# A planned conformer kernel on one core: own ends for the last two chunks, VectorE's score tiles by one PSUM bank at a time, and background before products

## The chip, the cores and the metric

The kernel runs on one core of a Trainium2 chip. The metric is the device time of one execution in microseconds (us). Each kernel was executed several times; all runs quoted here (none was over 1.5% above the fastest of its kernel) can be compared with each other. The span of a profile is a little shorter than the device time of the same run (1026.3 against 1028.1 us for the kernel before).

Engines are named as the profile names them: PE (matmuls), PEld (PE's weight loads), DVE (VectorE), ACT (ScalarE), POOL (GpSimd), SP (its queue issues the stores).

## The reference

One conformer block on two sequences of 4000 tokens of width 144, four heads of 36, all in bf16:

```python
h = silu(layernorm(x) @ w_ff1a) @ w_ff1b;      x = x + 0.5 * h
q, k, v = split(layernorm(x) @ w_qkv)                       # 4 heads of 36
p = softmax(einsum('bhqd,bhkd->bhqk', q, k) * 36 ** -0.5)   # 4000 x 4000 per head
x = x + einsum('bhqk,bhkd->bhqd', p, v) @ w_o
a, b = split(layernorm(x) @ w_pw1);            h = a * sigmoid(b)
c = depthwise_conv_of_5_taps(h, dw);           x = x + silu(c) @ w_pw2
h = silu(layernorm(x) @ w_ff2a) @ w_ff2b;      x = x + 0.5 * h
return layernorm(x)
```

## The kernel before

The tokens are cut into 16 chunks of 500 (eight per sequence). The attention of a chunk walks over 63 key tiles of 64 rows, so there are 1008 score tiles. One score tile has four heads times 64 keys times 500 queries; it fills two PSUM banks (128 x 1000 numbers), and its exponential is the main work of the kernel. Everything else is called background here: the first half of a chunk (`pre`: feed-forward 1, q, k, v), and the second half (`post1`: output projection and gate; `post2`: convolution, feed-forward 2, last LayerNorm, store).

The important fact about this program is that its order is decided when it is built. A small list scheduler in Python keeps a clock for each engine, with an estimated cost for each instruction. It picks the next step, emits it, and in the end writes one fixed instruction stream per engine, with semaphores. I call that the plan. A step that the plan puts at a wrong moment stays there: the engine waits in its queue.

Six PSUM banks serve scores and background; two hold the attention's accumulators. `KEEP = 2` keeps two pairs of banks for ScalarE's score tiles. The parts that the change and the argument touch, with cuts marked:

```python
    NXN, NXT, NTH, NHT, NSW = 5, 5, 4, 3, 2      # NSW: buffers of the convolution's result
    KEEP = 2; DSLACK = 0.6; BMIN = 1.5; DRAIN = 0.6; DGAP = 5.0

    def post2(c):                                  # the second half's end, one generator per chunk
        last = c % CPB == CPB - 1
        z = yield need("pe", swp, cond=lambda: c in glu_done and (last or c + 1 in glu_done))
        ...                                        # convolution, pw2, LayerNorm, feed-forward 2, store

    def emit_S(n):                                 # one score tile: four 64x64 quadrants, two banks
        lo, hi = banks.take_pair()
        for p in range(2):
            for hh in range(2):
                op("pe", "matmul", PSV[64 * p:64 * p + 64, hi if hh else lo, 0:CH], ...)
        return lo, hi

    def dve_tile(n, lo, hi):                       # exp on VectorE, by integer operations
        z = yield need("dve", dzp, hold=True)
        for hh, bk in ((0, lo), (1, hi)):
            op("dve", "tensor_scalar", ZB[:, z, hh, :], PSV[:, bk, 0:CH], ...)
            banks.give(bk)
        ...                                        # six more steps over 128 x 1000, the last writes PT

    # pick(): which step PE gets next; o = products with V, s = scores, ok = background that fits
        if R.kind == "q" and o and (not s or ts + 0.3 < deadline):
            return o[0]
        if ok:
            return min(ok, key=lambda q: not q[2].req.hold)
        ...

    def lag():                                     # background is behind: then no VectorE tile
        ...
        back = n // NT - 0.5 * (len(glu_done) + len(post_done))
        return back > BMIN + DRAIN * (NIT - n) / NT

    def reserve():                                 # while a VectorE tile is due, a third pair is kept
        ...
        return KEEP + 1 if due else KEEP

    # when the first sequence's keys are there:
            for par in range(2):
                S.add(series(post2(c) for c in range(par, NCH, 2)), R.last, rank=2)
```

So a VectorE tile needed a whole pair beside ScalarE's two, and the second halves ran in two series: chunks 0, 2, ..., 14 and chunks 1, 3, ..., 15.

The softmax here doesn't subtract the row's maximum and nothing guards it: scores larger than these inputs give would overflow.

Of the kernel before, what the change touches and what calls it, by code (L numbers as in the profile page):

```python
# [23 lines left out]
CH = 500  # L24
KT_ROWS = 64
# [211 lines left out]
need = Req  # L237
# [71 lines left out]
def bass_standalone__conformer_family_zipformer__speech_kernel(  # L309
# [16 lines left out]
    NCH = N // CH  # L326
    CPB = T // CH
# [4 lines left out]
    R = Rec(nc)  # L332
# [3 lines left out]
    def sb(name, shape, dt=BF16):  # L336
        return nc.alloc_sbuf_tensor(name, [128] + list(shape), dt)

    NXN, NXT, NTH, NHT, NSW = 5, 5, 4, 3, 2
    NPT = 7  # L340
    NU = 5
    NAN = 5
# [3 lines left out]
    NPRE = 2  # L346
    KEEP = 2
    DSLACK = 0.6
    PRELAG = 0.5
    BMIN = 1.5  # L350
    DRAIN = 0.6
    LATE = 0.3
    DGAP = 5.0
    MAXQ = 3
    DVE_EXP = True
    VG = 7
# [564 lines left out]
    def series(gens):  # L921
        for g in gens:
            yield from g
# [26 lines left out]
    group_left = {c: NT for c in range(NCH)}  # L950
    o_count = {c: 0 for c in range(NCH)}

    def emit_S(n):
        c, t = its[n]
        b = c // CPB
        k0, q0 = t * KT_ROWS, c * CH
        lo, hi = banks.take_pair()
        kcs = {min(k0 // CH, CPB - 1), min((k0 + KT_ROWS - 1) // CH, CPB - 1)}
        for p in range(2):
            for hh in range(2):  # L960
                bk = hi if hh else lo
                op("pe", "matmul", PSV[64 * p:64 * p + 64, bk, 0:CH],
                   lhsT=KT[64 * hh:64 * hh + 64, p, b, k0:k0 + KT_ROWS], rhs=QT[64 * hh:64 * hh + 64, p, q0:q0 + CH],
                   start=True, stop=True, skip_group_check=True,
                   r=[("WKT", b * CPB + kc) for kc in kcs] + [("WQT", c), "KTZ"], w=[("ps", bk)], cost=0.0525,
                   kind="q", lat=0.2)
        return lo, hi

    def emit_exp(n, lo, hi):
# [4 lines left out]
        banks.give(hi)  # L974
        pend.append((n, pt))

    def dve_tile(n, lo, hi):
        z = yield need("dve", dzp, hold=True)
        for hh, bk in ((0, lo), (1, hi)):
            op("dve", "tensor_scalar", ZB[:, z, hh, :], PSV[:, bk, 0:CH], ATT_SCALE * LOG2E * 256.0, 127.5 * 256.0,  # L980
               op0=ALU.mult, op1=ALU.add, r=[("ps", bk), ("ZF", z)], w=[("ZB", z)], cost=c_dve(CH))
            banks.give(bk)
        zz = ZB[:, z, :, :].rearrange("p b n -> p (b n)")
        mm = MB[:, z, :, :].rearrange("p b n -> p (b n)")
        yield need("dve")
        op("dve", "tensor_scalar", mm, zz, 0xFF, 0x6400, op0=ALU.bitwise_and, op1=ALU.bitwise_or, r=[("ZB", z)],
           w=[("MB", z, 0)], cost=c_dve(2 * CH, 4))
        op("dve", "tensor_scalar", zz, zz, 1, 0x7F80, op0=ALU.logical_shift_right, op1=ALU.bitwise_and,
           r=[("ZB", z), ("MB", z, 0)], w=[("EB", z)], cost=c_dve(2 * CH, 4))
        yield need("dve")  # L990
        v = E2A / (2 * E2B)
        op("dve", "tensor_scalar", MBH[:, z, :], MBH[:, z, :], 1.0 / 256, v - 4.5, op0=ALU.mult, op1=ALU.add,
           r=[("MB", z, 0)], w=[("MB", z, 1)], cost=c_dve(2 * CH, 4))
        yield need("dve")
        op("dve", "tensor_tensor", MBH[:, z, :], MBH[:, z, :], MBH[:, z, :], op=ALU.mult, r=[("MB", z, 1)],
           w=[("MB", z, 2)], cost=c_dve(2 * CH, 2))
        yield need("dve")
        op("dve", "tensor_scalar", MBH[:, z, :], MBH[:, z, :], E2B, 1.0 - E2B * v * v, op0=ALU.mult, op1=ALU.add,
           r=[("MB", z, 2)], w=[("MB", z, 3)], cost=c_dve(2 * CH, 4))
        pt = yield need("dve", ptp)  # L1000
        op("dve", "tensor_tensor", PT[:, pt, :, :].rearrange("p b n -> p (b n)"), ZBF[:, z, :], MBH[:, z, :],
           op=ALU.mult, r=[("MB", z, 3), ("EB", z)], w=[("PT", pt), ("MB", z, 0), ("EB", z), ("ZF", z)], cost=c_dve(2 * CH, 2))
        dzp.give(z)
        pend.append((n, pt))
        live_dve[0] -= 1
# [55 lines left out]
    def pick():  # L1061
        cands = []
        ts = s_start()
        if ts is not None:
            cands.append((ts, "S", None))
        if eq and ptp.free and (len(silu_done) >= NSILU or NSILU == 0):
            n, lo, hi = eq[0]
            te = max(R.free["act"], R.ready(("ps", lo), "act"), R.ready(("ps", hi), "act"), ptp.best() + 0.045)
            cands.append((te, "E", None))
        os = [(o_start(m), m) for m in pend]  # L1070
        os = [(t, m) for t, m in os if t is not None]
        if os:
            t, m = min(os, key=lambda q: (q[0], q[1]))
            cands.append((t, "O", m))
        for th in S.threads:
            t = S.start_of(th)
            if t is not None:
                cands.append((t, "T", th))
        if not cands:
            assert banks.keep > 0, "nothing can go on"  # L1080
            banks.keep -= 1
            return pick()
        tmin = min(q[0] for q in cands)
        soon = [q for q in cands if q[0] <= tmin + 0.1]
        other = [q for q in soon if not (q[1] in "SO" or (q[1] == "T" and q[2].req.eng == "pe"))]
        pe = [q for q in cands if (q[1] in "SO" or (q[1] == "T" and q[2].req.eng == "pe"))]
        pemin = min((q[0] for q in pe), default=1e9)
        if other and (min(q[0] for q in other) <= pemin or pemin > tmin + 0.1):
            e = [q for q in other if q[1] == "E"]
            a = [q for q in other if q[1] == "T" and q[2].req.eng == "act"]  # L1090
            d = [q for q in other if q[1] == "T" and q[2].req.eng != "act"]
            if d:
                return min(d, key=lambda q: (not q[2].req.hold, q[2].rank))
            if a:
                return a[0]
            return e[0]
        near = [q for q in pe if q[0] <= pemin + PW]
        o = [q for q in near if q[1] == "O"]
        bg = [q for q in near if q[1] == "T"]
        s = [q for q in near if q[1] == "S"]  # L1100
        deadline = act_end() - 0.48
        if ts is not None:
            limit = max(deadline, ts) + (LATE if lag() else 0.0)
        else:
            limit = 1e9
        ok = [q for q in bg if max(q[0], R.free["pe"]) + q[2].req.dur + 0.095 * (R.kind != q[2].req.kind) + 0.095 <= limit]
        if R.kind == "q" and o and (not s or ts + 0.3 < deadline):
            return o[0]
        if ok:
            return min(ok, key=lambda q: not q[2].req.hold)  # L1110
        if s:
            return s[0]
        if o:
            return o[0]
        if ts is not None:
            return (ts, "S", None)
        return min(pe, key=lambda q: q[0])

    def want_dve(n):
        c, t = its[n]  # L1120
        if not DVE_EXP or live_dve[0] >= 1 or t > NT - 6 or (t < 3 and c == 0) or len(kv_done) < CPB:
            return False
        return len(eq) + banks.pairs() >= KEEP and R.free["dve"] < R.free["pe"] + DSLACK and not lag()

    last_dve = [0.0]
    front = [0.0, 0]
# [10 lines left out]
        back = n // NT - 0.5 * (len(glu_done) + len(post_done))  # L1137
        return back > BMIN + DRAIN * (NIT - n) / NT

    def reserve():  # L1140
        n = n_s[0]
        if n >= NIT or not DVE_EXP or len(kv_done) < CPB:
            return KEEP
        c, t = its[n]
        due = (live_dve[0] < 1 and t <= NT - 6 and R.free["dve"] < R.free["pe"] + DSLACK
               and R.free["pe"] > last_dve[0] + DGAP and not lag())
        return KEEP + 1 if due else KEEP

    while n_s[0] < NIT or eq or pend or live_dve[0]:
        if mode["front"] and len(kv_done) == CPB:  # L1150
            mode["front"] = False
            front[:] = [0.0, n_s[0]]
            S.add(setup_dw())
            for par in range(NPRE):
                S.add(series(pre(c, False) for c in range(CPB + par, NCH, NPRE)), R.last)
            for par in range(2):
                S.add(series(post2(c) for c in range(par, NCH, 2)), R.last, rank=2)
        banks.keep = reserve()
        t, k, v = pick()
        if k == "S":  # L1160
            n = n_s[0]
            n_s[0] += 1
            lo, hi = emit_S(n)
            if want_dve(n):
                stats["dve"] += 1
                live_dve[0] += 1
                last_dve[0] = R.free["pe"]
                S.add(dve_tile(n, lo, hi), R.last, first=True, rank=3)
            else:
                eq.append((n, lo, hi))  # L1170
        elif k == "E":
            emit_exp(*eq.pop(0))
        elif k == "O":
            pend.remove(v)
            emit_O(v)
        else:
            S.run(v)
# [43 lines left out]
```

## Time and profile before

The kernel before took 1030.56 us (median of 4 runs, 1030.09 to 1031.57). From the page of its profile: the span, busy time of each engine with its share, then groups of instructions (output from input, shapes, count; busy us and mean ns of one; idle time before them and what ended most of it), then the stores:

```profile
span 1026.3 us, 26612 instructions
...
PE 924.8 (90%) x11294; PEld 365.0 (36%) x11294; DVE 788.0 (77%) x2092; ACT 945.8 (92%) x1175; POOL 283.3 (28%) x562
...
L158 ACT ACTIVATE PT<-PS 128x1000 bf16<-128x1000 f32 x914 | 851.9, 1041 | 11.5 <-PE PS L158 9.8
L158 PE MATMUL PS<-QT,KT 64*64 64x500 bf16 x4032 | 397.4, 391 | 50.3 <-ACT PT L158 29.5
L158 DVE TENSOR_SCALAR ZB<-PS 128x500 uint16<-128x500 f32 x188 | 118.5, 672 | 33.2 <-PE PS L158 31.9
...
out_dram<-XN SPq DMA_DIRECT2D x13, 140.6 KB
out_dram<-XN SPq DMA_DIRECT2D x6, 70.3 KB
```

There are 914 exponentials on ScalarE. 852 us of busy time over 914 is 0.93 us for one in a row. VectorE read 188 half tiles out of PSUM, so it took 94 of the 1008 score tiles. Of the stores, 13 are of whole chunks and six of half chunks. The plan stores by halves only where it finishes a chunk's last feed-forward after the attention, so six halves mean that the feed-forwards of three chunks, 13, 14 and 15, ended after it.

Busy time by stretch, the second row up to the end of the last exponential and the third from there on (columns: stretch, its length, then busy us of PE, PEld, DVE, ACT and POOL with the count of instructions, PE's granted clock, share of the DMA engines, GB/s):

```profile
110.00:160.00 50.00, 44.67 (x544) 16.60 (x541) 40.76 (x115) 46.58 (x58) 15.68 (x30) 1.00 0.01 2
500.00:966.99 466.99, 428.48 (x5363) 159.43 (x5364) 366.38 (x895) 463.83 (x567) 127.04 (x251) 1.00 0.02 5
966.99:1026.32 59.33, 37.43 (x229) 23.98 (x226) 27.63 (x110) 16.59 (x31) 13.97 (x34) 0.64 0.03 8
```

Up to 966.99 us ScalarE is nearly always busy: 463.83 of 466.99 us in the long stretch. Behind that come 59.33 us in which no engine is full on average (PE is busy for 37.43 us) and PE's clock is at 0.64 on average. I call these 59.33 us the end. PE is not the limit before the end; the list of waits (total us, times, longest us) has its weight loads waiting for exponentials to free banks:

```profile
PEld PS L158 <- ACT PT L158: 268.2, 543, 1.1
```

Six lines of the timeline that show chunks in the end (start, length, instruction): the convolution (`PS<-U,DG`) of 13; the first part of 13's feed-forward (`PS<-XT,WA`); the convolution of 14; the last matmuls of 13's feed-forward (`PS<-WB,HT`); the convolution of 15 and its feed-forward, the last one:

```profile
965.63 0.77 PE L158 MATMUL PS<-U,DG 128*128 128x500 bf16 x6
...
982.53 2.70 PE L158 MATMUL PS<-XT,WA 72*128 72x500 bf16 x6
985.03 1.35 PE L158 MATMUL PS<-U,DG 128*128 128x500 bf16 x6
...
990.90 0.79 PE L158 MATMUL PS<-WB,HT 128*125 128x144 bf16 x10
...
1003.69 1.62 PE L158 MATMUL PS<-U,DG 128*128 128x500 bf16 x12
...
1012.31 3.52 PE L158 MATMUL PS<-XT,WA 72*128 72x500 bf16 x8 [0.68 <-ACT XT L158]
```

Chunk 15 convolves 18.7 us after 14, and its feed-forward at 1012.31 us has the core to itself.

| | before |
|---|---|
| device time | 1030.56 us |
| exponentials on ScalarE / score tiles on VectorE | 914 / 94 |
| end of the last exponential | 966.99 us |
| the end (from there to the end of the span) | 59.33 us |

### The profile page before, as it was taken

The page shows a single profiled execution, that of the slowest core. Times are in us where ns is not written, and L with a number is a line of the kernel's source. Part 1 is how long each engine was busy: PE and PEld are TensorE (multiplying, and loading weights), DVE is VectorE, ACT ScalarE, POOL GpSimd, SP SyncE. Part 2 cuts the span into 40 slices and gives each one's busy share as a digit, 9 for nine tenths or more (in the row PEclk, how much of TensorE's full clock was granted, in tenths as well). Part 3 has the DMA queues.
Part 4 walks back from the last instruction along what each step waited for, and adds up shares of the span by engine and source line. Part 5 has one row for each costly group of instructions (what it writes and reads, how often), then busy time and mean ns, then how long its engine had stood idle before and what let it go on. Part 6 is the DMA issues. An engine that isn't in the chain of part 4 may idle for free.

```text
span 1026.3 us, 26612 instructions
## 1 busy us (share of the span) xinstructions
PE 924.8 (90%) x11294; PEld 365.0 (36%) x11294; DVE 788.0 (77%) x2092; ACT 945.8 (92%) x1175; POOL 283.3 (28%) x562
## 2 busy tenths in 40 slices
PE   7899989998999999998999999999999988998775
PEld 4444333333334333433333332333333333343343
DVE  6976877888966987787888778968886987666843
ACT  3899999999999999999999999999999999999741
POOL 3321313114324333320422132321513212223222
PEclk9999999999999999999999999999999999999956
DMA  4000000000000000000000000000000000000000
GB/s 130 3 1 2 2 2 2 1 2 2 1 2 2 2 2 2 7 2 2 2 7 2 7 7 2 2 8 7 8 2 8 2 7 7 2 8 7 7 6 12
DMA packets 7419, 7.31 MB, mean 7 GB/s; under 512 B 2349, under 2 KB 7300, under 8 KB 7300
## 3 DMA queue, kind: packets, MB, share of 16 engines
q1 hardware_dynamic: 6144, 5.14, 1.7%
q8 instruction: 88, 1.44, 0.6%
q10 hardware_dynamic: 1156, 0.47, 0.2%
q14 instruction: 31, 0.25, 0.1%
HBM read 3.31 MB, written 2.30 MB: 5 GB/s over the span
## 4 chain that ended last, share of the span: by engine, by line
ACT 65%; PE 22%; DVE 9%; POOL 2%; issue 1%; DMA 1%; ACTq 0%; POOLq 0%; DVEq 0%
ACT PT L158 59%; PE PS L158 22%; ACT TH L158 5%; DVE ZB L158 2%; DVE ST L158 1%; DVE MB L158 1%; DVE HT L158 1%; POOL RS L158 1%; DVE X L158 1%; POOL XN L158 1%; DMA WQKV<-in_w_qkv_dram 1%; DVE XT L158 1%; DVE PT L158 0%; DVE XN L158 0%; DVE MV L158 0%
## 5 line engine op out<-in xcount | busy, mean ns | idle before, releaser
L158 ACT ACTIVATE PT<-PS 128x1000 bf16<-128x1000 f32 x914 | 851.9, 1041 | 11.5 <-PE PS L158 9.8
L158 PE MATMUL PS<-QT,KT 64*64 64x500 bf16 x4032 | 397.4, 391 | 50.3 <-ACT PT L158 29.5
L158 PE MATMUL PS<-PT,VA 64*37 64x500 bf16 x4032 | 366.1, 373 | 10.5 <-ACT PT L158 7.0
L158 POOL TENSOR_SCALAR RS<-MV 125x4 f32<-125x4 f32 (+1 forms) x160 | 46.3, 289 | 668.3 <-DVE MV L158 662.7
L158 PEld LDWEIGHTS PS<-QT,KT 64*64 64x64 bf16 x4032 | 116.8, 103 | 306.5 <-ACT PT L158 219.9
L158 DVE TENSOR_SCALAR ZB<-PS 128x500 uint16<-128x500 f32 x188 | 118.5, 672 | 33.2 <-PE PS L158 31.9
L158 PEld LDWEIGHTS PS<-PT,VA 64*37 64x37 bf16 x4032 | 105.7, 95 | 71.9 <-ACT PT L158 42.7
L158 POOL TENSOR_SCALAR XN<-X,RS 125x144 bf16<-125x144 bf16 x228 | 127.6, 572 | 5.9
L158 ACT ACTIVATE TH<-PS 128x500 bf16<-128x500 f32 (+2 forms) x195 | 103.6, 538 | 8.0 <-PE PS L158 7.7
L158 DVE SCALAR_TENSOR_TENSOR HT<-TH,PS 128x500 bf16<-128x500 bf16 (+1 forms) x135 | 82.3, 618 | 32.4 <-ACT TH L158 31.5
L158 DVE SCALAR_TENSOR_TENSOR X<-PS,X 125x288 bf16<-125x288 f32 x128 | 56.9, 452 | 58.0 <-PE PS L158 57.3
L158 POOL TENSOR_TENSOR RS<-RS,NHALF 125x4 f32<-125x4 f32 (+1 forms) x103 | 97.6, 948 | 8.6
L158 PE MATMUL PS<-XT,WA 72*128 72x500 bf16 x256 | 77.7, 402 | 5.7 <-DVE HT L158 2.3
L158 DVE TENSOR_SCALAR MB<-MB 128x1000 f16<-128x1000 f16 x188 | 78.0, 415 | 1.5
L158 DVE BATCH_NORM_STATS2 ST<-X 125x6 f32<-125x144 bf16 x320 | 75.2, 294 | 0.4
L158 DVE TENSOR_TENSOR PT<-ZB,MB 128x1000 bf16<-128x1000 bf16 x94 | 66.0, 702 | 2.2
L158 DVE TENSOR_TENSOR MB<-MB 128x1000 f16<-128x1000 f16 x94 | 63.8, 679 | 2.1
L158 PE MATMUL PS<-WB,HT 128*125 128x144 bf16 x640 | 63.1, 241 | 2.5 <-ACT HT L158 1.5
L158 PEld LDWEIGHTS PS<-WB,HT 128*125 128x125 bf16 x640 | 49.4, 143 | 37.4 <-issue 22.6
L158 PE MATMUL PS<-IDENT,XN 125*72 125x125 bf16 x512 | 44.1, 226 | 15.0 <-DVE XN L158 11.7
L158 DVE COPY XT<-PS 72x1000 bf16<-72x1000 bf16 (+1 forms) x65 | 40.1, 617 | 11.7 <-PE PS L158 10.6
L158 PEld LDWEIGHTS PS<-IDENT,XN 125*72 125x72 bf16 x512 | 32.4, 115 | 40.8 <-DVE XN L158 15.2
(78 smaller groups left out, 682.0 us busy)
## 6 DMA issues: line engine op xcount, KB each, us to landing
X<-in_x_dram SPq DMA_DIRECT2D x16, 140.6 KB
out_dram<-XN SPq DMA_DIRECT2D x13, 140.6 KB
out_dram<-XN SPq DMA_DIRECT2D x6, 70.3 KB
WA<-in_w_ff1a_dram ACTq DMA_DIRECT2D x1, 144.0 KB
WB<-in_w_ff1b_dram ACTq DMA_DIRECT2D x1, 144.0 KB
WA<-in_w_ff2a_dram SPq DMA_DIRECT2D x1, 144.0 KB
WB<-in_w_ff2b_dram SPq DMA_DIRECT2D x1, 144.0 KB
WQKV<-in_w_qkv_dram ACTq DMA_DIRECT2D x1, 121.5 KB
```

The source lines that it names most:

```text
L158: ins = getattr(eng, o.name)(*o.a, **o.k)
```

## The change

The intent has two parts. First, chunks 14 and 15 no longer stand in the series but have ends of their own, with a third buffer. Second, a VectorE tile no longer takes a pair of banks: it asks for one bank, has two quadrants of the product made, reads it, gives it back, and does the same for the other half. The test of when a tile is due moves to a function of its own, and the reserve of a third pair goes. The distance `DGAP` falls from 5.0 to 4.0 us and changes its role: before, it only decided when the third pair was kept; now it is a condition of the tile itself. The diff also has a third thing, which the short description leaves out: a condition `OFREE`. With three or more PT buffers (exponentials for the products) free, background that fits goes to PE **before** a product. I call it the background-first rule. The core of the diff:

```diff
-    NXN, NXT, NTH, NHT, NSW = 5, 5, 4, 3, 2
+    NXN, NXT, NTH, NHT, NSW = 5, 5, 4, 3, 3
...
+    ALONE = 2
+    OFREE = 3
...
-    DGAP = 5.0
+    DGAP = 4.0
...
-    def dve_tile(n, lo, hi):
-        z = yield need("dve", dzp, hold=True)
-        for hh, bk in ((0, lo), (1, hi)):
+    def dve_tile(n):
+        z = None
+        for hh in range(2):
+            bk = yield need("pe", banks, dur=0.21, kind="q")
+            scores(n, hh, bk, 0.105)              # two of the four quadrants
+            if hh == 0:
+                z = yield need("dve", dzp, hold=True)
+            else:
+                yield need("dve", hold=True)
             op("dve", "tensor_scalar", ZB[:, z, hh, :], PSV[:, bk, 0:CH], ...)
             banks.give(bk)
...
-        if R.kind == "q" and o and (not s or ts + 0.3 < deadline):
+        if R.kind == "q" and o and (not s or ts + 0.3 < deadline) and not (ok and len(ptp.free) >= OFREE):
             return o[0]
...
-    def reserve():
-        ...
-        return KEEP + 1 if due else KEEP
+    def due():
+        ...
+        return (t <= NT - 7 and c in q_done and all(c // CPB * CPB + cc in kv_done for cc in range(CPB))
+                and R.free["dve"] < R.free["pe"] + DSLACK and R.free["pe"] > last_dve[0] + DGAP)
...
-                S.add(series(post2(c) for c in range(par, NCH, 2)), R.last, rank=2)
-        banks.keep = reserve()
+                S.add(series(post2(c) for c in range(par, NCH - ALONE, 2)), R.last, rank=2)
+            for c in range(NCH - ALONE, NCH):
+                S.add(post2(c), R.last, rank=2)
+        if due():
+            ...                                   # start dve_tile(n) as the next score tile
+        banks.keep = KEEP
```

More of the change, by code (lines that the diff above doesn't have):

```diff
@@ L951, in bass_standalone__conformer_family_zipformer__speech_kernel, with scores @@
     o_count = {c: 0 for c in range(NCH)}
-    def emit_S(n):
+    def scores(n, hh, bk, cost):
         c, t = its[n]
@@ L956, in emit_S @@
         k0, q0 = t * KT_ROWS, c * CH
-        lo, hi = banks.take_pair()
         kcs = {min(k0 // CH, CPB - 1), min((k0 + KT_ROWS - 1) // CH, CPB - 1)}
         for p in range(2):
-            for hh in range(2):
-                bk = hi if hh else lo
-                op("pe", "matmul", PSV[64 * p:64 * p + 64, bk, 0:CH],
-                   lhsT=KT[64 * hh:64 * hh + 64, p, b, k0:k0 + KT_ROWS], rhs=QT[64 * hh:64 * hh + 64, p, q0:q0 + CH],
-                   start=True, stop=True, skip_group_check=True,
-                   r=[("WKT", b * CPB + kc) for kc in kcs] + [("WQT", c), "KTZ"], w=[("ps", bk)], cost=0.0525,
-                   kind="q", lat=0.2)
+            op("pe", "matmul", PSV[64 * p:64 * p + 64, bk, 0:CH],
+               lhsT=KT[64 * hh:64 * hh + 64, p, b, k0:k0 + KT_ROWS], rhs=QT[64 * hh:64 * hh + 64, p, q0:q0 + CH],
+               start=True, stop=True, skip_group_check=True,
+               r=[("WKT", b * CPB + kc) for kc in kcs] + [("WQT", c), "KTZ"], w=[("ps", bk)], cost=cost, kind="q",
+               lat=0.2)
+    def emit_S(n):
+        lo, hi = banks.take_pair()
+        scores(n, 0, lo, 0.0525)
+        scores(n, 1, hi, 0.0525)
         return lo, hi
@@ L1117, in pick @@
         return min(pe, key=lambda q: q[0])
-    def want_dve(n):
-        c, t = its[n]
-        if not DVE_EXP or live_dve[0] >= 1 or t > NT - 6 or (t < 3 and c == 0) or len(kv_done) < CPB:
-            return False
-        return len(eq) + banks.pairs() >= KEEP and R.free["dve"] < R.free["pe"] + DSLACK and not lag()
     last_dve = [0.0]
@@ L1138, in lag @@
         return back > BMIN + DRAIN * (NIT - n) / NT
-    def reserve():
+    def due():
         n = n_s[0]
-        if n >= NIT or not DVE_EXP or len(kv_done) < CPB:
-            return KEEP
+        if n >= NIT or not DVE_EXP or len(kv_done) < CPB or live_dve[0] >= 1 or lag():
+            return False
         c, t = its[n]
-        due = (live_dve[0] < 1 and t <= NT - 6 and R.free["dve"] < R.free["pe"] + DSLACK
-               and R.free["pe"] > last_dve[0] + DGAP and not lag())
-        return KEEP + 1 if due else KEEP
+        return (t <= NT - 7 and c in q_done and all(c // CPB * CPB + cc in kv_done for cc in range(CPB))
+                and R.free["dve"] < R.free["pe"] + DSLACK and R.free["pe"] > last_dve[0] + DGAP)
     while n_s[0] < NIT or eq or pend or live_dve[0]:
@@ L1156, in bass_standalone__conformer_family_zipformer__speech_kernel @@
             for par in range(2):
-                S.add(series(post2(c) for c in range(par, NCH, 2)), R.last, rank=2)
-        banks.keep = reserve()
+                S.add(series(post2(c) for c in range(par, NCH - ALONE, 2)), R.last, rank=2)
+            for c in range(NCH - ALONE, NCH):
+                S.add(post2(c), R.last, rank=2)
+        if due():
+            n = n_s[0]
+            n_s[0] += 1
+            stats["dve"] += 1
+            live_dve[0] += 1
+            last_dve[0] = R.free["pe"]
+            S.add(dve_tile(n), R.free["pe"] - 0.3, first=True, rank=3)
+        banks.keep = KEEP
         t, k, v = pick()
@@ L1163, in bass_standalone__conformer_family_zipformer__speech_kernel @@
             lo, hi = emit_S(n)
-            if want_dve(n):
-                stats["dve"] += 1
-                live_dve[0] += 1
-                last_dve[0] = R.free["pe"]
-                S.add(dve_tile(n, lo, hi), R.last, first=True, rank=3)
-            else:
-                eq.append((n, lo, hi))
+            eq.append((n, lo, hi))
         elif k == "E":
```

## The prediction

> **What bounds the kernel now.** From 90 us to 961 us it is ScalarE: in the table of busy time by stretch it is busy 858 of 871 us, with 8 us of waits for PE. Its work is 914 exponentials of 128x1000, 852 us together (groups of instructions): 0.93 us each. PE looks 92% busy, but in the list of waits its weight loads wait 268 us for exponentials to free banks, so PE is not the limit on average. VectorE is about 80% busy; it takes 94 of the 1008 score tiles. One costs it 4.3 us (two PSUM reads at 0.67, six steps of 0.41 to 0.70). In the trace a tile lasts 5.3 us (median) from first read to product, but the next starts 3.3 us (mean) after that end: a tile every 9.0 us. Part of that gap is a wait for a whole free pair of banks beside the two kept for ScalarE, part a hold while other work lags.
>
> From 967 us on comes the end of chunks 13, 14 and 15, where the chain of waits is mostly PE at clock 0.50. Chunk 15's second half stands in series behind chunk 13: 13's last residual is at about 993 us, 15's convolution runs only at 1003.7, and its feed-forward alone fills 1012 to 1020.
>
> **What the change does.**
> 1. Own ends for 14 and 15 and a third SW buffer: 15's convolution can start when 14's does, at 985. But PE was already 100% busy at half clock from 980 to 990, so most of 15's PE work (about 10 us at clock 0.5) is moved, not hidden; it fills the PE gap at 992 to 996 and the latency chain that 15 now walks alone (1006 to 1012). The Trainium skill, "TensorE: Matmul & The Clock Gate", Part 1, says the clock is half after an idle window and full after sustained work; this trace shows 0.50 in most of the end, so denser work may bring some full clock. I count 10 us (8 to 13).
> 2. Tiles one bank at a time: no wait for a pair, each bank back after 0.67 us, and the next tile due 4.0 us after the last, not 5.0. I expect a tile every 8 to 8.5 us: 98 to 112 tiles, about 104. Each takes 0.93 us off ScalarE: 9 us. VectorE rises to about 84%.
> 3. Added: half products use two quadrants at a time. The skill's "TensorEngine Tiling (Array Packing)", Tiling Modes, has 64x64 as four independent tiles; here four take 0.41 us and eight 0.62, so 0.21 us per set; two halves cost 0.42. With 104 tiles that is 22 us more PE, nearly all in time PE waits for ScalarE. I charge 2 us of new ScalarE gaps.
> 4. Background goes before products where three PT buffers are free: with the finer interleaving I guess 5 us.
>
> **Prediction.** 1030.8 - 10 - 9 + 2 - 5 = 1009 us; 8 in 10 between 998 and 1020. Faster by over 2%: 0.54; same: 0.44; slower: 0.02.
>
> **What would show it.** About 904 exponentials on ScalarE, 104 on VectorE; ScalarE still over 98% busy in the middle; the tile gap down to 2 to 2.5 us; last exponential to the end about 50 us, the convolutions of 14 and 15 adjacent.
>
> **What would make it wrong.** Tiles held back by lag instead of banks (no more of them); ScalarE starved by single banks (under 97%); the end bound by PE at half clock (gain 5 us), or warm (gain 17 us).

## The result, and the profile after

The changed kernel took 1013.79 us (median of 4 runs, 1012.16 to 1015.19); the kernel before took 1030.56 us in the same rounds. The ratio is 0.9835, with a 95% interval of 0.9818 to 0.9853. By the threshold of 2% this counts as the same. Here and below, a ratio is the mean time of one kernel's fast runs over that of the other's fast runs of the same rounds, so it is not quite the ratio of the medians quoted.

The page after, the same lines:

```profile
span 1010.4 us, 26729 instructions
...
PE 920.5 (91%) x11294; PEld 400.8 (40%) x11294; DVE 824.1 (82%) x2160; ACT 932.0 (92%) x1163; POOL 288.8 (29%) x563
...
L158 ACT ACTIVATE PT<-PS 128x1000 bf16<-128x1000 f32 x906 | 841.0, 1054 | 13.4 <-PE PS L158 12.0
L158 PE MATMUL PS<-QT,KT 64*64 64x500 bf16 x4032 | 419.9, 387 | 28.2 <-ACT PT L158 22.2
L158 DVE TENSOR_SCALAR ZB<-PS 128x500 uint16<-128x500 f32 x204 | 137.7, 675 | 54.0 <-PE PS L158 50.1
...
out_dram<-XN SPq DMA_DIRECT2D x14, 140.6 KB
out_dram<-XN SPq DMA_DIRECT2D x4, 70.3 KB
```

There are 906 exponentials and 102 tiles on VectorE. And there are 14 whole stores and four halves: **chunk 13's feed-forward is no longer in the end** (only its last LayerNorm and its store are, side by side with chunk 15's first steps).

Busy time by stretch, cut at this kernel's last exponential:

```profile
110.00:160.00 50.00, 45.16 (x519) 18.16 (x518) 41.55 (x114) 42.31 (x52) 16.80 (x28) 0.90 0.01 2
500.00:964.65 464.65, 421.01 (x5333) 171.23 (x5324) 383.64 (x902) 459.67 (x557) 114.74 (x218) 1.00 0.02 4
964.65:1010.35 45.70, 27.35 (x184) 18.50 (x182) 22.89 (x93) 11.69 (x23) 11.54 (x28) 0.66 0.04 10
```

The span went from 1026.32 to 1010.35 us, 15.97 us less. It divides as follows.

- The end: 59.33 to 45.70 us, **13.6 us less**.
- Up to the last exponential: 966.99 to 964.65 us, **2.3 us less**. ScalarE's busy time up to there fell from 929.2 to 920.3 us (the sums of the busy column over all stretches up to the last exponential), 8.9 us less. Its idle time rose from 37.8 to 44.3 us. So three quarters of what the tiles saved was lost again, and 4.3 us of that lies between 110 and 160 us (46.58 busy before, 42.31 after).

In the timeline, the last matmuls of 13's feed-forward now run beside the last exponential (964.65 us). In the end, the convolutions of 14 and 15 stand side by side (24 matmuls in one piece), followed by two feed-forwards:

```profile
964.35 0.53 PE L158 MATMUL PS<-WB,HT 128*125 128x144 bf16 x5
...
981.20 4.88 PE L158 MATMUL PS<-U,DG 128*128 128x500 bf16 x24 [1.33 <-POOL U L158]
...
992.12 3.52 PE L158 MATMUL PS<-XT,WA 72*128 72x500 bf16 x8 [0.68 <-ACT XT L158]
...
999.50 1.86 PE L158 MATMUL PS<-XT,WA 72*128 72x500 bf16 x8
```

PE's waits for ScalarE's banks shrank. That PE has more work is not what this shows: they are 206.6 us in e4 below, where PE's work is not increased.

```profile
PEld PS L158 <- ACT PT L158: 202.3, 435, 1.6
```

And one VectorE tile in each timeline, by its reads of PSUM, before and after:

```profile
954.95 1.26 DVE L158 TENSOR_SCALAR ZB<-PS 128x500 uint16<-128x500 f32 x2 [0.52 <-PE PS L158]
```

```profile
952.42 0.68 DVE L158 TENSOR_SCALAR ZB<-PS 128x500 uint16<-128x500 f32 x1 [0.18 <-PE PS L158]
...
954.49 0.68 DVE L158 TENSOR_SCALAR ZB<-PS 128x500 uint16<-128x500 f32 x1
```

Before, the two reads follow each other. After, the second waits for its own bank and its own half product. Over all tiles, computed from the starts and ends in the two traces, the second read starts 0.60 us after the first before and 1.44 us after it afterwards (medians). A tile lasts 5.3 and 6.6 us from first read to product (medians). The pause until the next tile is 3.3 and 1.2 us, the distance of tiles 9.0 and 8.3 us (means). The typical distance hardly changed (medians 7.7 and 7.6 us): the mean fell because the long distances went (the longest is 35.9 us before, 16.6 us after).

### The profile page after: what moved, and what is told of

The parts are those of the page before. It is cut to its first block, busy times and chain, and to the rows that moved or that the text cites. A ratio compares the mean times of both kernels' runs of the same rounds, so it can differ in the third digit from the quotient of the medians.

```text
span 1010.4 us, 26729 instructions
## 1 busy us (share of the span) xinstructions
PE 920.5 (91%) x11294; PEld 400.8 (40%) x11294; DVE 824.1 (82%) x2160; ACT 932.0 (92%) x1163; POOL 288.8 (29%) x563
## 3 DMA queue, kind: packets, MB, share of 16 engines
q8 instruction: 88, 1.44, 0.6%
## 4 chain that ended last, share of the span: by engine, by line
ACT 47%; PE 33%; DVE 12%; POOL 6%; issue 1%; DMA 1%; ACTq 0%; POOLq 0%; DVEq 0%
ACT PT L158 41%; PE PS L158 33%; ACT TH L158 6%; POOL XN L158 3%; POOL RS L158 3%; DVE MB L158 2%; DVE ZB L158 2%; DVE ST L158 2%; DVE X L158 1%; DVE HT L158 1%; DVE XT L158 1%; DMA WQKV<-in_w_qkv_dram 1%; DVE MV L158 1%; DVE PT L158 0%; DVE OTF L158 0%
## 5 line engine op out<-in xcount | busy, mean ns | idle before, releaser
L158 ACT ACTIVATE PT<-PS 128x1000 bf16<-128x1000 f32 x906 | 841.0, 1054 | 13.4 <-PE PS L158 12.0
L158 PE MATMUL PS<-QT,KT 64*64 64x500 bf16 x4032 | 419.9, 387 | 28.2 <-ACT PT L158 22.2
L158 PE MATMUL PS<-PT,VA 64*37 64x500 bf16 x4032 | 355.5, 376 | 16.5 <-ACT PT L158 13.3
L158 POOL TENSOR_SCALAR RS<-MV 125x4 f32<-125x4 f32 (+1 forms) x159 | 50.1, 315 | 643.1 <-DVE MV L158 637.8
L158 PEld LDWEIGHTS PS<-QT,KT 64*64 64x64 bf16 x4032 | 125.5, 104 | 225.8 <-ACT PT L158 146.6
L158 DVE TENSOR_SCALAR ZB<-PS 128x500 uint16<-128x500 f32 x204 | 137.7, 675 | 54.0 <-PE PS L158 50.1
L158 PEld LDWEIGHTS PS<-PT,VA 64*37 64x37 bf16 x4032 | 114.9, 95 | 132.1 <-ACT PT L158 49.1
L158 DVE TENSOR_SCALAR MB<-MB 128x1000 f16<-128x1000 f16 x204 | 84.7, 415 | 1.7
L158 DVE TENSOR_TENSOR PT<-ZB,MB 128x1000 bf16<-128x1000 bf16 x102 | 70.6, 692 | 2.4
L158 DVE TENSOR_TENSOR MB<-MB 128x1000 f16<-128x1000 f16 x102 | 69.0, 676 | 2.1
```

What stands on the lines that cost most here:

```text
L158: ins = getattr(eng, o.name)(*o.a, **o.k)
```

## The experiments

Twelve kernels ran, all with correct results. In the table, tiles are VectorE's score tiles, "last exp" is the end of the last exponential in the profiled run, and "end" the time from there to the end of the span. Each ratio is to the kernel before in the same rounds (its median was 1029.07 to 1029.58 us there). How far two single profiles can differ is shown by e2, which has the instruction order of the changed kernel: 1.8 us in the last exponential, 0.1 us in the end.

| kernel | median us | ratio (95%) | tiles | last exp | end | half stores |
|---|---|---|---|---|---|---|
| before | 1030.56 | 1 | 94 | 966.99 | 59.33 | 6 |
| changed | 1013.79 | 0.9835 (0.9818 to 0.9853) | 102 | 964.65 | 45.70 | 4 |
| e1: before + own ends | 1022.35 | 0.9925 (0.9911 to 0.9940) | 94 | 968.65 | 52.62 | 6 |
| e2: changed - own ends | 1013.73 | 0.9844 (0.9829 to 0.9858) | 102 | 966.44 | 45.76 | 4 |
| e3: changed - rule | 1016.90 | 0.9870 (0.9850 to 0.9889) | 95 | 970.14 | 46.23 | 4 |
| e4: before + rule | 1016.70 | 0.9890 (0.9862 to 0.9918) | 106 | 967.22 | 47.16 | 4 |
| e5: before, background forced | 1026.47 | 0.9969 (0.9946 to 0.9993) | 88 | 978.26 | 46.23 | 4 |
| e6: before - reserve | 1022.82 | 0.9947 (0.9926 to 0.9969) | 84 | 973.41 | 47.11 | 6 |
| e7: changed, measured costs | 1005.96 | 0.9778 (0.9761 to 0.9794) | 104 | 957.92 | 45.26 | 4 |
| e8: changed, filled end | 1010.32 | 0.9821 (0.9806 to 0.9836) | 102 | 964.35 | 45.56 | 4 |
| e9: changed, nudged | 1018.32 | 0.9892 (0.9873 to 0.9912) | 100 | 972.15 | 46.18 | 4 |
| e10: e7, nudged | 1013.93 | 0.9850 (0.9835 to 0.9865) | 101 | 966.85 | 44.82 | 4 |
| e11: e4, measured costs | 1015.40 | 0.9872 (0.9853 to 0.9892) | 104 | 966.44 | 46.88 | 6 |
| e12: before, measured costs | 1033.82 | 1.0042 (1.0027 to 1.0057) | 95 | 971.10 | 60.76 | 6 |

### e1 and e2: are the separate ends what shortened the end?

e1 adds the ends to the kernel before and nothing else; e2 takes them out of the changed kernel.

```diff
# e1, on the kernel before            # e2 is the reverse, on the changed kernel
-    NXN, NXT, NTH, NHT, NSW = 5, 5, 4, 3, 2
+    NXN, NXT, NTH, NHT, NSW = 5, 5, 4, 3, 3
-                S.add(series(post2(c) for c in range(par, NCH, 2)), R.last, rank=2)
+                S.add(series(post2(c) for c in range(par, NCH - 2, 2)), R.last, rank=2)
+            for c in range(NCH - 2, NCH):
+                S.add(post2(c), R.last, rank=2)
```

> The kernel before with only the separate ends for chunks 14 and 15 (and the third SW buffer). Everything up to the last exponential is the same program, so 94 VectorE tiles, 914 exponentials, last exponential at 967 us as before. Theory P (the prediction's term 1): the 59.3 us after the last exponential shrink by 8 to 13 us, total 1018 to 1023. Theory R (rival: in the changed kernel the end is short mainly because chunk 13 was finished before the attention ended, not because of the separate ends): chunk 13's feed-forward still lies in the end here, and PE at half clock has the same work to do, so the end shrinks by 3 to 7 us only, total 1024 to 1028.

> The changed kernel with the separate ends undone (14 and 15 again in the two series, two SW buffers). Theory P: it loses what the ends gave, 8 to 13 us, total about 1024. Theory R: its instruction order is the same on every engine, because the chain that held 15 (chunk 13's second half) is through before 15 may start; so 1014 within 2 us, end 45 to 47 us as in the changed kernel.

Measured: e1 gains 0.75% and its end is 52.62 us, 6.7 us shorter, in the range of theory R (3 to 7 us) and below that of theory P (8 to 13). Its total of 1022.35 us is in theory P's range (1018 to 1023), so e1 alone does not decide between them. Its stores are still 13 and six, so chunk 13 is in the end. The stretch from its last exponential on, and its stores:

```profile
968.65:1021.27 52.62, 34.20 (x229) 22.93 (x227) 27.83 (x111) 15.55 (x31) 13.86 (x34) 0.70 0.03 9
```

```profile
out_dram<-XN SPq DMA_DIRECT2D x13, 140.6 KB
out_dram<-XN SPq DMA_DIRECT2D x6, 70.3 KB
```

e2 loses nothing (0.9844 against 0.9835, the intervals overlap). A comparison of the two programs shows the same instructions in the same order on every engine. They differ only in which of the convolution's result buffers is used. So **in the changed kernel the separate ends do nothing at all**. They let 15 start beside 13, but 13 is already through when 15 could start. By difference, the 13.6 us of the end are 6.7 us for 15's wait behind 13 (e1) and 6.9 us for having 13's work out of the end as well (52.62 to 45.70 us).

### e3 and e4: which part brings tiles, and which moves chunk 13 out of the end?

```diff
# e3, on the changed kernel (e4 adds the same condition, with 3 for OFREE, to the kernel before)
-        if R.kind == "q" and o and (not s or ts + 0.3 < deadline) and not (ok and len(ptp.free) >= OFREE):
+        if R.kind == "q" and o and (not s or ts + 0.3 < deadline):
```

> The changed kernel without the one condition that lets background work on PE go before a product when three or more PT buffers are free. Theory P (that rule is worth a few us, the single banks bring the tiles): 99 to 104 VectorE tiles, total 1012 to 1019. Theory R (the rule, not the single banks, brings the tiles and the earlier background): tiles fall to about 95, exponentials about 913, the last exponential ends after 968, total 1020 to 1030.

> The kernel before with that one condition added and nothing else: tiles by pairs, series ends, gap 5.0. Theory P: 94 to 97 tiles, total 1024 to 1030. Theory R: tiles rise to about 106, the last exponential ends at 960 to 966, chunk 13 is finished by then or nearly so, total 1010 to 1018, as good as the whole change.

Measured: the tiles follow the rule. Without it the single banks give 95 tiles, hardly more than the 94 of before; with it alone, by pairs, there are 106. So theory R was right about the tiles (e4's last exponential, at 967.22 us, came a little later than it said). But it was wrong about e3's time, which it put at 1020 to 1030: e3 took 1016.90 us, in theory P's range, because its end is short too (46.23 us, 14 whole stores). The rule alone, and single banks with the own ends and the 4.0 us but without the rule, each move chunk 13 out of the end and take the total to about 1017 us. Having all brings 1013.79 us, a further 3 us, which is less than a mere shuffle of the plan moves (e9).

What the tiles bring by themselves is seen up to the last exponential. These are the stretches from 0 to there, of the kernel before, the changed kernel and e4:

```profile
0.00:966.99 966.99, 887.40 (x11067) 341.07 (x11068) 760.40 (x1982) 929.23 (x1145) 269.38 (x528) 1.00 0.03 7
0.00:964.65 964.65, 893.20 (x11113) 382.26 (x11114) 801.20 (x2067) 920.31 (x1141) 277.21 (x535) 0.99 0.03 7
0.00:967.22 967.22, 878.69 (x11104) 372.31 (x11105) 811.97 (x2098) 918.04 (x1137) 278.72 (x535) 1.00 0.03 7
```

In e4 twelve more tiles take 11.2 us off ScalarE's busy time, and its idle time grows by 11.4 us (37.8 to 49.2), so the last exponential ends where it did before. All that e4 gains is in the end. And since e4 has no half products, they are not needed for such new idle time; in e3, which has them but not the rule, the idle time is 42.6 us.

### e5 and e6: is it the missing chunk that shortens the end, and what held it up?

e5 changes one constant of the kernel before: the plan calls background late sooner, and refuses VectorE tiles while it is. e6 takes away only the third pair reserved for a due tile.

```diff
# e5, on the kernel before
-    BMIN = 1.5
+    BMIN = 1.0
# e6, on the kernel before
-        return KEEP + 1 if due else KEEP
+        return KEEP
```

> The kernel before with one constant changed (BMIN 1.5 to 1.0): the plan forces background work sooner and refuses VectorE tiles while it lags; pairs, series ends and product-first order stay. Theory E (the end after the last exponential is short in every variant in which chunk 13's second half is finished by then, whatever does it): the end falls from 59 to 45 to 48 us; VectorE gets fewer tiles (about 88, so some 920 exponentials) and the last exponential ends at 974 to 980, total 1018 to 1026. Rival T (the end is short because of the single banks or of the rule themselves, for instance by leaving a better order of threads at the switch): the end stays above 53 us, and with fewer tiles the total is 1030 or more.

> The kernel before without the third bank pair that is held back from background work while a VectorE tile is due. Theory B (this reserve, not the tile's own use of two banks, is what kept background work waiting in the kernel before, and single banks help because they need no reserve): VectorE tiles fall to about 84 (about 924 exponentials), but chunk 13 is nearly through at the last exponential, the end is 45 to 50 us and the last exponential ends at 972 to 980; total 1018 to 1028. Rival: the reserve cost background nothing; then the end stays at 57 to 60 us and the total is 1034 to 1042, since 10 tiles more lie on ScalarE.

Measured: e5's end is 46.23 us, with neither single banks, nor rule, nor separate ends; theory T falls. It is paid for with six tiles, and the last exponential is 11 us later, so the total hardly gains (0.31%; 1026.47 us is just above what theory E said). e6 is the most telling: it has ten tiles **fewer** than the kernel before, and ScalarE is busy for 6.0 us more up to the last exponential (935.2 against 929.2 us), and yet it is 0.53% faster. Its last exponential comes 6.4 us later and its end is 12.2 us shorter. The stretches from the last exponential on, e5 and then e6:

```profile
978.26:1024.49 46.23, 28.18 (x176) 19.30 (x176) 20.27 (x79) 12.28 (x24) 12.98 (x32) 0.62 0.03 10
```

```profile
973.41:1020.52 47.11, 31.49 (x204) 21.29 (x203) 24.93 (x97) 14.32 (x28) 12.30 (x30) 0.63 0.03 10
```

In e6 chunk 13 still has stores by halves; its last feed-forward matmuls run from 980.0 to 982.6 us, seven to nine microseconds after the last exponential, before chunk 15's LayerNorms have anything for PE to do. That is soon enough (e11 does the same). This is what theory B said: the reserve of a third pair, which served a VectorE tile that waited for a pair, kept banks from background, and single banks need no reserve. But a rival stands. Without the reserve there are also fewer tiles, and e5 shows that fewer tiles with background forced free chunk 13 as well. So that the reserve is how single banks help is likely, not shown; nor is what they add by holding a bank for a shorter time.

### e7: are ScalarE's new idle times stalls of the plan?

In the changed kernel ScalarE loses 4.3 us between 110 and 160 us. The timeline there shows how:

```profile
121.42 2.54 POOL L158 TENSOR_SCALAR XN<-X,RS 125x144 bf16<-125x144 bf16 x4
...
124.01 0.63 PE L158 MATMUL PS<-IDENT,XN 125*72 125x125 bf16 x8 [1.90 <-POOL XN L158]
...
126.25 0.59 ACT L158 ACTIVATE TH<-PS 128x500 bf16<-128x500 f32 x1 [1.91 <-PE PS L158]
...
129.78 0.63 PE L158 MATMUL PS<-QT,KT 64*64 64x500 bf16 x4 [0.69 <-ACT PT L158]
```

GpSimd normalises a chunk until about 124 us. PE has the transpositions of that chunk next in its queue and stands still; ScalarE runs out of scores. The Trainium skill, "TensorE: Matmul & The Clock Gate", Part 2, says that only weight loads are pulled ahead and that "the MATMULs themselves stay in program order"; the 1.90 us agree. Between 122.1 and 125.4 us PE runs nothing but these eight transpositions, 0.63 us of them. Then the clock falls to half for 10.2 us (125.7 to 135.9 us in the trace): four score quadrants take 0.63 us at 129.78 us instead of 0.41.

The plan underrates these GpSimd operations: it has 0.7 us for a power of 125x4, which takes 1.13 us on average in the trace of the kernel before. e7 gives the plan measured durations:

```diff
-  r=[("VE", u), "NHALF"], w=[("RS", u)], cost=0.7)
+  r=[("VE", u), "NHALF"], w=[("RS", u)], cost=1.1 if n > 2 else 0.72)
# likewise 0.25 to 0.3 for the operation before it, and 0.2 to 0.24 and 0.3 for the convolution's diagonal weights on VectorE
```

> The changed kernel, its plan given measured durations for four operations that it underrates (the power of 125x4 on GpSimd 1.1 us, of 125x2 0.72, the op before it 0.3, the diagonal weights on VectorE 0.24 and 0.3). Theory S (ScalarE's 5 us of extra idle between 110 and 160 us come from PE, in program order, standing at a transposition that the plan placed before GpSimd had its input, and from the half clock that followed): ScalarE's idle time between 110 and 160 us falls from 7.7 to 3 to 5 us, no half-clock stretch near 125 us, about 104 tiles, total 1007 to 1012. Rival (such stalls arise anywhere, the plan only moves them): ScalarE's idle time before the last exponential stays at 38 to 42 us, total 1012 to 1017.

Measured: 1005.96 us, the best of all, faster by 2.2% than the kernel before, and below the range of either theory. But the expected reason is wrong. In the stretch from 110 to 160 us ScalarE is no busier than in the changed kernel (42.52 against 42.31 us):

```profile
110.00:160.00 50.00, 44.30 (x540) 19.83 (x538) 42.55 (x118) 42.52 (x55) 16.10 (x30) 0.97 0.01 2
```

The stall has moved. PE now stands for 2.42 us at another matmul that the plan put too early, this time waiting for VectorE:

```profile
128.36 2.42 PE L158 MATMUL PS<-WB,HT 128*125 128x144 bf16 x20 [2.42 <-DVE HT L158]
```

So the rival was right that the plan only moves such stalls: ScalarE's idle time before the last exponential is 40.1 us, within its 38 to 42. Its total (1012 to 1017 us) was not met. The gain lies elsewhere: two more tiles, and less idle time before 110 us (25.7 against 27.5 us) and between 160 and 500 us (1.8 against 4.2 us).

### e8: is the half clock what the end costs?

e8 fills PE's planned waits in the end with 33 matmuls of constant weights into a bank that the attention has left. That bank is thereby kept from background in the end, a second difference.

```diff
+ if eng == "pe" and mode["tail"]:          # st: when the next matmul's inputs are ready, by the plan
+     for _ in range(int((st - R.free["pe"] - 0.3) / 0.3)):
+         R.op("pe", "matmul", PSV[:, BX + 1, 0:CH], lhsT=WA1[0:HD, 0, 0:128], rhs=WA1[0:HD, 0, 0:CH], ...)
```

> The changed kernel, with 33 idle matmuls (constant weights, into the bank that the attention has left) put where the plan sees PE waiting after the attention; results unchanged. Theory C (the half clock of PE costs the end: it is 0.5 for some 33 of the 46 us and PE is busy for about 20 of them): clock 1.00 in most of the end, the end 38 to 42 us instead of 46, total 1006 to 1010. Rival L (the end is a chain of latencies, the clock matters little or the added matmuls stand in the way): the end is 44 us or more, total 1012 to 1016.

Measured: the end is 45.56 against 45.70 us, so rival L's figure came true. But the test is weaker than meant, for the clock did not stay up. Two stretches of the end, the changed kernel first, then e8:

```profile
970.00:975.00 5.00, 1.58 (x12) 1.37 (x12) 4.36 (x19) 0.08 (x1) 2.65 (x6) 0.50 0.01 2
980.00:985.00 5.00, 3.80 (x18) 2.45 (x19) 0.84 (x2) 0.92 (x2) 0.50 (x5) 0.50 0.02 5
```

```profile
970.00:975.00 5.00, 3.67 (x27) 1.90 (x28) 3.64 (x15) 0.67 (x2) 2.08 (x5) 1.00 0.09 29
980.00:985.00 5.00, 5.00 (x22) 2.80 (x21) 0.41 (x2) 0.48 (x2) 0.50 (x5) 0.50 0.02 5
```

From 970 to 975 us the fill holds the clock at 1.00, when PE has little to do. From 980 to 985 us, where the convolutions are, it is 0.50 in both. What a full clock would be worth in the end is therefore still open. The median of 1010.32 us looks better than 1013.79 us, but the ratios (0.9821 and 0.9835) lie within each other's intervals.

### e9 to e12: how much is merely another shuffle of the plan?

e9 nudges a constant that has nothing to do with the change; e10 is e7 with the same nudge. e11 gives the measured costs to e4, and e12 to the kernel before.

```diff
# e9 on the changed kernel, e10 on e7
-    PW = 0.12
+    PW = 0.125
```

> The changed kernel with a constant of the plan nudged without any reason (the window in which candidates for PE count as equally early, 0.12 to 0.125 us), to see how much a merely reshuffled plan moves the time. Theory N (reshuffling is worth several us, so differences of 3 to 5 us between these variants say little): it differs from the changed kernel's ratio of 0.9835 by 0.3 to 0.8 points either way. Rival: the plan is stable, ratio within 0.2 points (1011.5 to 1015.5 us). In either case the end is 45 to 47 us, for chunk 13 is through.

> The plan with measured durations, the same nudge. Theory M (measured durations are themselves worth some 7 us, as between the changed kernel and the run with measured costs): 5 to 9 us less than the nudged kernel of this call. Rival N (that gain was a lucky reshuffle): within 4 us of it, or slower.

> The kernel before, with the background-first rule and the measured durations, but tiles by pairs and series ends. Theory D (single banks are dispensable once the rule lets background go first): about 104 tiles, end 45 to 48 us, ratio to the kernel before 0.977 to 0.983. Rival (the single banks still bring 3 us or more on top, as between the rule alone and the whole change): ratio 0.983 to 0.990.

> The kernel before with the measured durations alone. Theory M: some 5 to 9 us faster by fewer stalls of PE, ratio 0.991 to 0.995, with chunk 13 still unfinished at the last exponential and an end of 55 to 60 us. Rival (the kernel before had been tuned together with its wrong durations, so right ones only reshuffle it): ratio 0.997 to 1.006.

Measured: the nudge alone costs the changed kernel 0.57 points of the ratio, 5.9 us. The ends of e9 and e10 stay at 46.18 and 44.82 us; nearly all the difference lies before the last exponential. Theory N holds. Measured costs gain 0.57 points without the nudge, 0.42 with it (4.4 us by the medians of the same rounds, between the 5 to 9 of theory M and the rival's 4), 0.18 on the rule alone, and lose 0.42 in the kernel before, in the range of the rival there. So they are no reliable gain, and e7 is partly luck. For e11 the rival's range was met: the rule without single banks reaches 0.9872. Single banks beside the rule, against the rule alone, stand at 0.9835 (0.9892 with the nudge) against 0.9890, and with measured costs at 0.9778 (0.9850 with the nudge) against 0.9872. That is anything from nothing to 0.9 points, about as much as a shuffle moves, so their worth beside the rule is not settled.

## Why the prediction was right or wrong

The time, 1013.79 us, lies inside the range of 998 to 1020 and 4.8 us above the prediction, in part by luck, as the steps show. The more probable class (faster by over 2%, 0.54) was not met; the ratio stayed at 0.9835. Step by step:

1. **Own ends, 10 us (8 to 13). The step failed, though its size looks right.** The end did get shorter, by 13.6 us, and the convolutions of 14 and 15 are adjacent as forecast. But the named cause contributes nothing in the changed kernel (e2), and 6.7 us where it acts alone (e1). The prediction took the end's content as given: it read that 15 waits for 13, and did not ask whether the other parts of the change would still leave 13 there. In its place the runs showed that the end is 44.8 to 47.2 us wherever the last matmul of chunk 13's feed-forward ends between 3.3 us before and 9.3 us after the last exponential (changed, e2 to e11), and 52.6 to 60.8 us in the three where it ends 23.9 to 26.2 us after it (before, e1, e12).
2. **Tiles one bank at a time, about 104 tiles, 9 us. The count was right, the cause only in part.** There are 102 tiles, 8.3 us apart; 8 tiles of 0.93 us are 7.5 us, and ScalarE's busy time before the last exponential fell by 8.9 us. VectorE's share between 90 and 961 us is 84%, as forecast. But without the rule the single banks yield 95 tiles (e3), so it is not the wait for a pair that kept the number down. The test for background that is behind (`lag`) is the likely cause, since the long distances between tiles are what shrank; how often it refused a tile was not counted. The pause between tiles fell to 1.2 us, below the 2 to 2.5 forecast, and the tile itself grew by 1.3 us, which the sum did not have.
3. **Half products, 22 us more PE, 2 us of new ScalarE gaps. The first size was right, the second wrong.** The group of score matmuls grew from 397.4 to 419.9 us, 22.5 us for the same number of matmuls, or 0.22 us for each of 102 tiles. Against e4, which has the rule too but no half products (389.9 us), it is 30 us. The Trainium skill's four independent 64x64 tiles ("TensorEngine Tiling (Array Packing)", Tiling Modes) agree with that: two at a time leave the other half idle. But ScalarE's idle time before the last exponential grew by 6.6 us, not by 2; the charge was mis-sized. This is where most of the tiles' gain went. ScalarE's share in the middle fell from 98.5% to 97.8%, below the 98% forecast. The stall at 124 us and the half clock after it are shown in the trace; that half products cause it is not, since e4, which has none, loses busy time in the same stretch too (42.52 us busy), and 11.4 us in all.
4. **Background before products, a guess of 5 us. Underrated where it stands alone.** Alone it is worth 1.1% (e4), most of what the whole change gives, all of it in the end. Taken out of the whole change it costs 3.1 us by the medians (e3). It raises the number of tiles to 106 and also takes chunk 13 out of the end. It was the line that I costed least, because the change's description does not mention it.

The sum of the parts before the last exponential was 12 us, of which 2.3 came. The end was 10, of which 13.6 came. Two errors partly cancelled. The effects do not add: ends 7 us, rule 13 us, single banks with ends 13 us, each measured against the kernel before, and 17 us together. The rule and the single banks both remove chunk 13 from the end, and the own ends help only while it is there.

What stays open: how much of the single banks' help is the absent reserve and how much the shorter hold of a bank; their true worth beside the rule; what the shorter distance of 4.0 us does; and what a full clock in the end would bring.

## What to carry to other kernels

Where background work hides behind a saturated engine, ask first what is left when that engine stops. Here one chunk too many after the last exponential cost 13 us, a variant with ten tiles fewer on VectorE was faster because it was gone, and a count of half stores hinted at it at a glance. The count alone does not decide: e6 and e11 have six half stores and short ends, because chunk 13 ended only 9 us late there. Test each part of a change both added alone and taken out: parts that remove the same wait look additive in a sum, and one of them can be dead weight. With an order planned at build time, nudge a constant that means nothing before believing a difference of a few us; here that moved the time by 5.9 us.

## What the Trainium skill lacked or had wrong

- "TensorE: Matmul & The Clock Gate", Part 1, says that the clock is full again after about 3.4 us of sustained work. In the kernel before PE was listed busy without a break from 980 to 990 us and stayed at 0.50 all that time, as this stretch shows. The half-clock stretches lasted 3.4 to 30.7 us in these runs, close to multiples of 3.4 us except where the end of the run cut them off, which does agree with the page's window. Why the clock stayed low is not settled here: the matmuls in that stretch use 72 to 128 rows, four of them (until 981.1 us) are transpositions, and their ends are modelled by the profile.

```profile
980.00:990.00 10.00, 10.00 (x53) 6.32 (x52) 1.37 (x3) 5.58 (x10) 0.50 (x5) 0.50 0.00 0
```
